# Two local attentions in one hand-ordered kernel: free tiles in place of a ring, first blocks in halves, new tables

## The chip, the core and the metric

One core of a Trainium2 chip runs the whole kernel. The metric is the device time of one execution in microseconds, as the median of several runs. TensorE multiplies matrices into PSUM, VectorE (DVE) and ScalarE (ACT) do elementwise work, GpSimd (POOL) masks and issues loads, SyncE (SP) issues DMAs.

## The reference

Two independent attention layers over 2048 positions and 1024 features, 32 heads of 32, whose outputs stand side by side. Layer A is dilated (8 keys, every second position), layer B a sliding window of 256 keys.

```python
def _A_ref(x, wqkv, wo):
    H = 32; W, dil = 8, 2
    q, k, v = heads(x @ wqkv)
    idx = pos[:, None] - (arange(W) * dil)[None, :]
    logits = einsum("bhsd,bhswd->bhsw", q, k[idx]) * Dh ** -0.5   # idx < 0 masked
    o = einsum("bhsw,bhswd->bhsd", softmax(logits), v[idx])
    return o.reshape(B, S, D) @ wo

def _B_ref(x, wqkv, wo):
    H = 32; W = 256
    q, k, v = heads(x @ wqkv)
    scores = einsum("bhqd,bhkd->bhqk", q, k) * Dh ** -0.5
    mask = (idx[:, None] - idx[None, :] >= 0) & (idx[:, None] - idx[None, :] < W)
    o = einsum("bhqk,bhkd->bhqd", softmax(where(mask, scores, -1e9)), v)
    return o.reshape(B, S, D) @ wo

return concatenate([a, b], axis=-1)
```

## The kernel before, in words

The work is cut into eight units of 512 positions: units 0 to 3 are layer B ("dense"), units 4 to 7 layer A ("window"), its even positions and its odd ones each in a row, so that the dilation is gone. A unit has eight head groups s of four heads. For each unit the kernel computes q and k of the eight groups (`qk_items`, L583), V in three parts (`v_items`, L648: one "wide" part of four groups and two parts of two), the attention of each group, and the output projection (`o_items`, L711), which runs during the next unit.

Everything is float32 through TensorE's rounded form: each operand is split into a high part and the low rest, and each product is three matmuls (`TERMS`). The split is made on the chip: `parts` casts the raw block to its high part on ScalarE (L208) or VectorE (L211), whichever the program expects to be done first, and subtracts for the low part on VectorE (L214).

**Blocks.** `Stream` holds a list of items, 512 KB each, in the order in which they are needed: x in four blocks of two tiles a unit, and the weights. The first six (`SIDE`) are loaded through SyncE, whole, and split in halves in an order written into `split_first`; the rest are loaded through GpSimd (L149) when one of three raw buffers falls free. Weights are split into a pool of three buffers, one or two blocks ahead of their use (`ahead`). In the wide part of V, four weight blocks are used one after the other for two column blocks b = 0 and 1; in dense units b = 1 runs two steps behind (`SKEW`). The split of the next block is begun with the first step of b = 1.

**Tiles.** x and the attention outputs `ot` share one pool of 19 tiles (`NX`) as a ring: each new tile takes the place of the one given out 19 tiles before (`Stream.tile`). Attention's values (`values_ready`, L835 and L1118) are not placed while that old tile is an output whose last projection hasn't run (`next_holds`).

**Attention of a dense group.** q and k leave PSUM as high and low parts (L520, L524) and six DMAs on SyncE scatter them into stacks of 96 rows, `qst` and `kst` (L544); k's last 256 positions go to HBM for the next unit (L534) and are read back there (L473). A first pass computes scores (L983), their maxima (L988) and sums (L993). Their logarithms go into rows 96 to 127 of the q stack (L1022, L1028), against ones in the same rows of the k stack, which `marks` writes once (L395). A second pass (L1067) gives probabilities by an exponential (L1074) and masks (L1052, L1055), and L1132 multiplies by V. Window groups have 64 small scores matmuls (L779), a softmax on VectorE and ScalarE (L787 to L830) and L851 for the values.

**The order of the work.** TensorE's order is written when the program is built. `Clock` models engines, queues and DMAs with fixed durations; the main loop at the end takes, at TensorE's modelled time, the first ready item of four lists: projections (`gemm`, with x's blocks as items of no cost), second passes, first passes and small ones. Tables steer it, one entry a unit. `V_AT` and `O_AT` say before which head group's q and k the parts of V and the projections of the unit before stand; `EDGES_V` says after how many steps at the end of a unit the next unit's blocks are split. `PACE` holds margins: for a dense unit the first number favours GpSimd for masks, the second is added to the modelled landing of k before scores may be placed, the third and fourth delay the second pass and the reuse of score banks, the fifth is added to the modelled cost of the values, the last says at which step of q and k the next weight is split:

```python
done["stack"][u, s] = max(e2, h2["hi"]) + PACE[u][1]
```

Constants are built at fixed modelled times: `turns` at 17, `keeps` at 23, `marks` (eight activations, four to each of the two k stacks) at 24, `nears` at 60. Ten warm-up matmuls (L1215) run before the first blocks land.

## Time and profile before

| | |
|---|---|
| median of 3 runs (lowest, highest) | 1802.55 us (1800.61, 1803.97) |
| the profiled execution | 1804.45 us |
| its span, first to last instruction | 1802.7 us |
| mean granted TensorE clock | 0.997 |
| GpSimd busy | 352.8 us (20%) |
| DMA, mean over the span | 143 GB/s, 257.52 MB |
| median from issue to landing, `raw` loads of wqk by GpSimd | 4.1 us |
| the same, k's scatter (`kst<-nat`) | 5.5 us |
| the same, the three whole x blocks on SyncE into `raw` | 7.5 us |

A row of the timeline gives start, duration, engine, line, operation, the tiles it writes and reads, shapes and count; in brackets stand the engine's idle time before it and what ended that. A row of waits gives who waited for whom, the total, the count and the longest. PE is TensorE, PEld its weight loads, which run beside it; SPq is SyncE's queue. Matmuls are pipelined and their ends modelled, so starts say more than durations.

### The profile page before, as it was taken

The page shows a single profiled execution, that of the slowest core. Times are in us where ns is not written, and L with a number is a line of the kernel's source. Part 1 is how long each engine was busy: PE and PEld are TensorE (multiplying, and loading weights), DVE is VectorE, ACT ScalarE, POOL GpSimd, SP SyncE. Part 2 cuts the span into 40 slices and gives each one's busy share as a digit, 9 for nine tenths or more (in the row PEclk, how much of TensorE's full clock was granted, in tenths as well). Part 3 has the DMA queues.
Part 4 walks back from the last instruction along what each step waited for, and adds up shares of the span by engine and source line. Part 5 has one row for each costly group of instructions (what it writes and reads, how often), then busy time and mean ns, then how long its engine had stood idle before and what let it go on. Part 6 is the DMA issues. An engine that isn't in the chain of part 4 may idle for free.

```text
span 1802.7 us, 39540 instructions
## 1 busy us (share of the span) xinstructions
PE 1778.2 (99%) x15210; PEld 1476.7 (82%) x15210; DVE 1270.3 (70%) x2757; ACT 1052.5 (58%) x2632; POOL 352.8 (20%) x759
## 2 busy tenths in 40 slices
PE   8999999999999999999999999999999999999999
PEld 6887888888788888888888888878888788888887
DVE  5778866649667678766667587787649576867783
ACT  5577676666666665757677455464525454644442
POOL 2111113232331212222242500110101000110000
PEclk9999999999999999999999999999999999999999
DMA  6555654546655556464545344444434443534432
GB/s 198 159 142 151 186 150 147 162 122 167 167 138 156 158 147 182 127 164 135 159 134 166 114 127 129 137 124 135 144 115 144 139 133 119 169 119 128 140 100 82
DMA packets 108860, 257.52 MB, mean 143 GB/s; under 512 B 14464, under 2 KB 29824, under 8 KB 108672
## 3 DMA queue, kind: packets, MB, share of 16 engines
q0 software_dynamic: 41760, 152.06, 28.3%
q1 hardware_dynamic: 57696, 86.15, 17.9%
q10 hardware_dynamic: 9216, 16.78, 2.5%
q8 instruction: 120, 1.97, 0.5%
q14 instruction: 68, 0.56, 0.1%
HBM read 164.63 MB, written 23.07 MB: 104 GB/s over the span
## 4 chain that ended last, share of the span: by engine, by line
PE 84%; DVE 6%; DMA 4%; ACT 3%; issue 2%; POOL 0%; SPq 0%; ACTq 0%; DVEq 0%; POOLq 0%
PE g L583 30%; PE g L711 14%; PE g L648 13%; PE s L1067 5%; PE x L583 5%; PE s L983 5%; PE x L711 4%; PE o L1132 3%; PE x L648 2%; DVE w L214 1%; PE s L779 1%; DMA halo<-nat 1%; ACT wide L827 1%; DMA kst<-nat 1%; DMA raw<-wqk 1%
## 5 line engine op out<-in xcount | busy, mean ns | idle before, releaser
L583 PE MATMUL g<-x,w 128*128 128x512 f32 x2640 | 659.7, 394 | 2.0 <-ACT w L208 1.6
L583 PEld LDWEIGHTS g<-x,w 128*128 128x128 f32 x2640 | 488.9, 189 | 96.5 <-ACT w L208 2.0
L988 DVE CUSTOM_DVE_ANT_0 s<-s,mask_d 128x384 f32<-128x384 f32 (+2 forms) x512 | 262.5, 555 | 133.0 <-PE s L983 132.3
L214 DVE TENSOR_TENSOR w<-raw,w 128x512 fp32r<-128x512 f32 x514 | 335.0, 694 | 25.3 <-ACT w L208 18.7
L648 PE MATMUL g<-w,x 128*128 128x256 f32 (+1 forms) x1920 | 347.6, 324 | 4.9 <-DVE w L214 3.1
L993 ACT ACTIVATE s<-s,nm 128x384 f32<-128x384 f32 (+2 forms) x512 | 273.7, 535 | 74.1 <-DVE nm L988 72.6
L648 PEld LDWEIGHTS g<-w,x 128*128 128x128 f32 x1920 | 286.9, 192 | 31.4 <-DVE w L214 5.4
L711 PE MATMUL g<-ot,w 128*128 128x512 f32 x1128 | 278.8, 392 | 0.0
L711 PEld LDWEIGHTS g<-ot,w 128*128 128x128 f32 x1128 | 208.8, 188 | 39.6 <-DVE ot L919 0.2
L1074 ACT ACTIVATE pbuf<-s 128x512 f32<-128x512 f32 (+1 forms) x368 | 189.3, 601 | 53.9 <-PE s L1067 46.3
L1052 POOL TENSOR_SCALAR_AFFINE_SELECT pbuf<-pbuf 128x256 f32<-128x256 f32 (+1 forms) x428 | 170.5, 425 | 212.3 <-ACT pbuf L1074 200.3
L211 DVE CAST w<-raw 128x1024 fp32r<-128x1024 f32 x191 | 136.9, 717 | 88.5 <-PE g L583 29.5
L149 POOL DMA_DIRECT2D raw<-wqk x126 | 69.1, 549 | 572.1 <-DVE w L214 341.3
L983 PE MATMUL s<-kst,qst 96*128 96x384 f32 (+2 forms) x512 | 144.2, 341 | 10.5 <-DMA halo<-nat 4.0
L1067 PE MATMUL s<-qst,kst 128*128 128x128 f32 (+2 forms) x704 | 128.5, 307 | 0.1
L827 ACT COPY wide<-wide 32x256 f32<-32x256 f32 x256 | 103.4, 404 | 34.1 <-DVE wide L818 30.4
L1067 PEld LDWEIGHTS s<-qst,kst 128*128 128x128 f32 x704 | 109.5, 189 | 16.8 <-ACT s L993 2.3
L983 PEld LDWEIGHTS s<-kst,qst 96*128 96x128 f32 x512 | 92.8, 190 | 33.9 <-ACT s L993 8.2
L993 ACT ACTIVATION_READ_ACCUMULATOR s<-s,nm 128x1 f32 x512 | 105.1, 205 | 0.1
L583 PE MATMUL x<-x,w 128*128 128x512 f32 x432 | 104.6, 394 | 0.0
L149 POOL DMA_DIRECT2D raw<-wv x72 | 46.7, 649 | 255.6 <-DVE w L214 131.3
L583 PEld LDWEIGHTS x<-x,w 128*128 128x128 f32 x432 | 80.0, 188 | 17.6 <-DVE w L214 0.4
(107 smaller groups left out, 1931.1 us busy)
## 6 DMA issues: line engine op xcount, KB each, us to landing
raw<-wqk POOLq DMA_DIRECT2D x126, 512.0 KB, 4.1
raw<-wv POOLq DMA_DIRECT2D x72, 512.0 KB, 4.3
raw<-wo POOLq DMA_DIRECT2D x64, 512.0 KB, 3.9
qst<-nat SPq DMA_DIRECT2D x96, 256.0 KB, 4.8
kst<-nat SPq DMA_DIRECT2D x96, 256.0 KB, 5.5
raw<-xs POOLq DMA_DIRECT2D x28, 512.0 KB, 4.9
outs<-ost ACTq DMA_DIRECT2D x56, 256.0 KB, 2.4
kst<-halo SPq DMA_DIRECT2D x72, 128.0 KB, 2.6
```

Source lines behind the costliest of these rows:

```text
L211: nc.vector.tensor_copy(t[:, 0, :], raw)
L214: nc.vector.tensor_tensor(t[:, 1, c:c + 512], raw[:, c:c + 512], t[:, 0, c:c + 512].bitcast(F32), op=ALU.subtract)
L583: nc.tensor.matmul(h["ps"], h["w"][:, a, k * P:(k + 1) * P], xt[u][k][:, b, :], start=(k == 0 and i == 0), stop=(k == NK - 1 and i == 2))
L648: nc.tensor.matmul(ps, xt[u][kw * g + k][:, a, p0:p0 + P], h["w"][g][:, c, k], start=(first and t == 0 and half == 0), stop=(last and t == 2),
L711: nc.tensor.matmul(h["ps"], w[:, a, c:c + P], ot[u, k][:, b, :], start=(k == 0 and i == 0), stop=(k == NK - 1 and i == 2))
L827: nc.scalar.copy(diag[r:r + 32, :, :, c:c + 32], pieces[r:r + 32, :, :, 1 + i % 2, :])
L983: nc.tensor.matmul(ps[:, :n], q[0:96, j, b * P:(b + 1) * P], kk[0:96, j, c0:c1], start=True, stop=True)
L988: nc.vector.tensor_tensor_reduce(ps[:, :n], ps[:, :n], mask[:, cut:full], scale=-1.0, scalar=BIG, op0=ALU.add, op1=ALU.min, accum_out=nm)
L993: nc.scalar.activation(ps[:, :n], ps[:, :n], AF.Exp, bias=nm, scale=-1.0, accum_out=sm)
L1052: nc.gpsimd.affine_select(w, w, pattern=[[0, m], [step, n]], compare_op=ALU.is_ge, fill=0.0, base=base, channel_multiplier=chan)
L1067: nc.tensor.matmul(ps[:, x:x + w], kk[:, j, 256 + kb * P:256 + (kb + 1) * P], q[:, j, q0:q0 + w], start=True, stop=True)
L1074: nc.scalar.activation(w, ps[:, :m * n].rearrange("p (j n) -> p j n", j=m), AF.Exp)
```

## The change

- `Tiles` replaces the ring: a list of free tiles. A tile of x is given back when its last matmul has been placed (`used` counts the steps that read it, 16 of q and k and 8 of V: `most`), a tile of `ot` with the last projection that reads it. `values_ready` asks for any free tile; an x item of units 1 to 7 for two.
- The twelve halves of the first six blocks are loaded one by one on SyncE, in the order `FIRST`, and `split_first` splits them in that order.
- `X_AT` lets the first blocks of the next unit's x stand ahead of a head group's q and k: in unit 0 block 0 before s = 6. (Unit 7 has an entry, but no next unit.)
- In the wide part of V, the split of the next weight begins with the first step of b = 0.
- The ones are written per k stack, at 5 and at 34 of the modelled time.
- `PACE`, `V_AT`, `O_AT` and `EDGES_V` get new entries.

```diff
...
+FIRST = ((0, 0), (1, 0), (0, 1), (2, 0), (3, 0), (3, 1), (4, 0), (1, 1), (4, 1), (2, 1), (5, 0), (5, 1))
+X_AT = ((6,), (), (), (), (), (), (), (6, 7))
...
-PACE = ((-0.2, 2.4, 0.1, 0.1, 0.0, -99, 4), (0.2, 1.2, 0.3, 0.1, 0.4, -99, 0), (0.1, 2.4, 0.3, 0.1, 0.0, -99, 0), (0.2, 1.2, 0.5, 0.4, 0.0, -99, 2), (6.0, 6.0, -0.5, 0.5, 1, 1), (4.0, 7.0, 1.5, 0.2, 1, 2), (4.0, 7.0, 0.5, 0.2, 1, 3), (4.0, 7.0, 0.5, 0.0, 1, 1))
-V_AT = ({0: 0, 4: 1, 7: 2}, {0: 0, 4: 1, 7: 2}, {0: 0, 5: 1, 7: 2}, {0: 0, 5: 1, 7: 2}, {1: 0, 5: 1, 7: 2}, {0: 0, 6: 1, 7: 2}, {0: 0, 5: 1, 7: 2}, {0: 0, 6: 1, 7: 2})
-O_AT = ({2: (0, 1), 3: (2, 3), 4: (4, 5), 5: (6, 7)}, {2: (0, 1), 3: (2, 3), 4: (4, 5), 5: (6, 7)}, {2: (0, 1), 3: (2, 3), 4: (4, 5), 5: (6, 7)}, {2: (0, 1), 3: (2, 3), 5: (4, 5), 6: (6, 7)}, {2: (0, 1), 3: (2, 3), 4: (4, 5), 6: (6, 7)}, {4: (0, 1), 5: (2, 3), 6: (4, 5), 7: (6, 7)}, {1: (0, 1), 2: (2, 3), 5: (4, 5), 6: (6, 7)}, {1: (0, 1), 2: (2, 3), 4: (4, 5), 5: (6, 7)})
+PACE = ((0.4, 2.4, 0.1, 0.1, 0.4, -99, 4), (0.1, 1.8, 0.3, 0.1, 0.4, -99, 2), (0.1, 0.6, 0.3, 0.1, 0.0, -99, 0), (0.2, 2.4, 0.3, 0.1, 0.0, -99, 0), (6.0, 8.0, 0.2, 0.5, 1, 1), (2.0, 6.0, 1.5, 0.2, 1, 2), (4.0, 7.0, 0.5, 0.2, 1, 3), (4.0, 7.0, -0.5, 0.0, 1, 1))
+V_AT = ({0: 0, 4: 1, 7: 2}, {0: 0, 3: 1, 7: 2}, {0: 0, 5: 1, 7: 2}, {0: 0, 5: 1, 7: 2}, {0: 0, 4: 1, 7: 2}, {0: 0, 6: 1, 7: 2}, {0: 0, 6: 1, 7: 2}, {0: 0, 6: 1, 7: 2})
+O_AT = ({2: (0, 1), 3: (2, 3), 4: (4, 5), 5: (6, 7)}, {3: (0, 1), 4: (2, 3), 5: (4, 5), 7: (6, 7)}, {2: (0, 1), 3: (2, 3), 4: (4, 5), 5: (6, 7)}, {2: (0, 1), 3: (2, 3), 4: (4, 5), 6: (6, 7)}, {3: (0, 1), 4: (2, 3), 5: (4, 5), 6: (6, 7)}, {2: (0, 1), 3: (2, 3), 4: (4, 5), 5: (6, 7)}, {1: (0,), 2: (1,), 3: (2, 3), 4: (4,), 5: (5,), 6: (6, 7)}, {1: (0,), 2: (1, 2), 3: (3, 4), 5: (5, 6), 6: (7,)})
...
-EDGES_V = (((2, 'k7'), (7, 'v0'), (14, 'x0'), (17, 'v1'), (17, 'q0'), (24, 'x1'), (28, 'x2'), (31, 'x3')), ((1, 'k7'), (4, 'x0'), (10, 'v0'), (11, 'v1'), (21, 'x1'), (23, 'x2'), (26, 'q0'), (31, 'x3')), ((2, 'k7'), (10, 'v0'), (14, 'v1'), (16, 'x0'), (22, 'x1'), (26, 'x2'), (26, 'q0'), (31, 'x3')), ((5, 'k7'), (7, 'v0'), (12, 'x0'), (17, 'v1'), (17, 'q0'), (18, 'x1'), (22, 'x2'), (26, 'x3')), ((2, 'k7'), (8, 'x0'), (10, 'v0'), (18, 'v1'), (20, 'x1'), (25, 'x2'), (26, 'q0'), (31, 'x3')), ((2, 'k7'), (7, 'v0'), (11, 'x0'), (14, 'v1'), (17, 'q0'), (18, 'x1'), (22, 'x2'), (26, 'x3')), ((0, 'k7'), (10, 'v0'), (11, 'x0'), (14, 'x1'), (15, 'v1'), (24, 'x2'), (29, 'q0'), (31, 'x3')), ((2, 'k7'), (7, 'v0'), (14, 'x0'), (17, 'v1'), (17, 'q0'), (21, 'x1'), (25, 'x2'), (29, 'x3')))
+EDGES_V = (((2, 'k7'), (5, 'v0'), (14, 'q0'), (17, 'x0'), (18, 'v1'), (27, 'x1'), (29, 'x2'), (33, 'x3')), ((1, 'k7'), (1, 'x0'), (10, 'v0'), (11, 'v1'), (20, 'x1'), (23, 'x2'), (32, 'q0'), (33, 'x3')), ((3, 'k7'), (10, 'v0'), (14, 'v1'), (15, 'x0'), (22, 'x1'), (26, 'x2'), (27, 'q0'), (31, 'x3')), ((5, 'k7'), (6, 'v0'), (12, 'x0'), (14, 'q0'), (17, 'v1'), (18, 'x1'), (24, 'x2'), (32, 'x3')), ((2, 'k7'), (5, 'x0'), (10, 'v0'), (16, 'v1'), (17, 'x1'), (22, 'x2'), (26, 'q0'), (28, 'x3')), ((0, 'k7'), (7, 'v0'), (13, 'x0'), (14, 'v1'), (17, 'q0'), (20, 'x1'), (26, 'x2'), (31, 'x3')), ((2, 'k7'), (10, 'x0'), (10, 'v0'), (15, 'v1'), (16, 'x1'), (26, 'x2'), (29, 'q0'), (33, 'x3')), ((2, 'k7'), (7, 'v0'), (14, 'x0'), (17, 'v1'), (17, 'q0'), (21, 'x1'), (25, 'x2'), (29, 'x3')))
...
+ONES_AT = 5.0, 34.0
...
+class Tiles:
+    def __init__(self, pool, ck):
+        self.pool, self.ck, self.free = pool, ck, list(range(NX))
+        self.seat, self.uses = {}, {}
+    def take(self, key, name="x"):
+        i = self.free.pop(0)
+        self.seat[key] = i
+        return self.pool.tile([P, 2, S], F32R, tag=f"x{i}", name=name)
+    def used(self, key, most):
+        n = self.uses[key] = self.uses.get(key, 0) + 1
+        if n == most:
+            self.ck.defer(self.ck.now + 0.2, lambda: self.free.append(self.seat[key]))
 class Stream:
...
-        self.ring = []
-        self.load_to(NRAW + len(more))
+        for i in range(SIDE):
+            self.raw[i] = (more[i] if i < len(more) else self.raws.tile([P, 1024], F32, tag="raw", name="raw")), [None, None]
+        for i, h in FIRST:
+            raw, ts = self.raw[i]
+            nc.sync.dma_start(raw[:, h * S:h * S + S], items[i][1][:, h, :] if items[i][0] == "x" else items[i][1][:, h * S:h * S + S])
+            ts[h] = ck.copy("half", ck.now)
+        self.loaded = SIDE
...
     def load_to(self, n):
...
-            early = self.loaded < SIDE
-            raw = self.more[self.loaded] if self.loaded < len(self.more) else self.raws.tile([P, 1024], F32, tag="raw", name="raw")
+            raw = self.raws.tile([P, 1024], F32, tag="raw", name="raw")
...
-            (self.nc.sync if early else self.nc.gpsimd).dma_start(raw if len(ap.shape) == 2 else raw.rearrange("p (a b) -> p a b", a=2), ap)
-            self.raw[self.loaded] = raw, (self.ck.copy if early else self.ck.fetch)("load", self.ck.now)
+            self.nc.gpsimd.dma_start(raw if len(ap.shape) == 2 else raw.rearrange("p (a b) -> p a b", a=2), ap)
+            self.raw[self.loaded] = raw, self.ck.fetch("load", self.ck.now)
...
-                    t = self.tile(None)
-                    self.ready[i].append(self.parts(t, raw[:, h * S:(h + 1) * S], t0, i < SIDE))
+                    t = self.seats.take(self.items[i][3] + (h,))
+                    self.ready[i].append(self.parts(t, raw[:, h * S:(h + 1) * S], t0, False))
...
-                self.ready[i] = self.parts(t, raw, t0, i < SIDE)
+                self.ready[i] = self.parts(t, raw, t0, False)
...
     def split_first(self):
...
-        for i, (kind, _, _) in enumerate(self.items[:SIDE]):
-            self.tiles[i] = [] if kind == "x" else self.wpool.tile([P, 2, 1024], F32R, tag="w", name="w")
+        for i in range(SIDE):
+            self.tiles[i] = [] if self.items[i][0] == "x" else self.wpool.tile([P, 2, 1024], F32R, tag="w", name="w")
...
-        for i, h in ((0, 0), (0, 1), (1, 0), (2, 0), (3, 0), (3, 1), (1, 1), (2, 1), (4, 0), (4, 1), (5, 0), (5, 1)):
+        for i, h in FIRST:
...
-                self.tiles[i].append(self.tile(None))
+                self.tiles[i].append(self.seats.take(self.items[i][3] + (h,)))
...
-            self.ready[i].append(self.parts(dst, raw[:, c], t, True))
+            self.ready[i].append(self.parts(dst, raw[:, c], t[h], True))
...
-    def tile(self, what):
-        self.ring.append(what)
-        return self.xpool.tile([P, 2, S], F32R, tag="x", name="x" if what is None else "ot")
-    def next_holds(self):
-        return self.ring[len(self.ring) - NX] if len(self.ring) >= NX else None
...
     def parts(self, t, raw, t0, side):
...
         for s in range(NG):
             if u and s in O_AT[u]:
...
+            plan += [("xe", u + 1, g) for g, at in enumerate(X_AT[u]) if at == s and u + 1 < U]
...
-        return [(at, keys.get(name) or ("x", u + 1, int(name[1]))) for at, name in (EDGES_V if with_v else EDGES_K)[EDGE_AT[u]]]
+        return [(at, keys.get(name) or ("x", u + 1, int(name[1]))) for at, name in (EDGES_V if with_v else EDGES_K)[EDGE_AT[u]]
+                if name[0] != "x" or int(name[1]) >= len(X_AT[u])]
...
+        elif p[0] == "xe":
+            unit_x(p[1], p[2])
...
+    most = [2 * NG + sum(n for _, n in parts_of(u)) for u in range(U)]
+    seats_x = Tiles(xpool, ck)
...
-    def marks():
+    def marks(t):
...
-        for t in kst:
-            for j in range(4):
-                nc.scalar.activation(t[96:P, j, :].rearrange("p (a s) -> p a s", s=P), zero, AF.Identity,
-                                     bias=heads[96:P, j:j + 1], scale=1.0)
-                ck.use("act", 0.73, ck.now)
+        for j in range(4):
+            nc.scalar.activation(t[96:P, j, :].rearrange("p (a s) -> p a s", s=P), zero, AF.Identity,
+                                 bias=heads[96:P, j:j + 1], scale=1.0)
+            ck.use("act", 0.73, ck.now)
...
+                seats_x.used(("x", u, k // 2, k % 2), most[u])
...
+            seats_x.used(("x", u, (kw * g + k) // 2, k % 2), most[u])
...
             if wide and r == 0:
-                if k == 0 and b == 1 and n < 3:
+                if k == 0 and b == 0 and n < 3:
...
+            if n == NG - 1:
+                seats_x.used(("ot", u, k), 1)
...
-        return [[(lambda: 0.0, lambda g=g: run(g), 0.0, lambda: None)] for g in range(4)]
+        def ready():
+            return 0.0 if not u or len(seats_x.free) > 1 else None
+        return [[(ready, lambda g=g: run(g), 0.0, lambda: None)] for g in range(4)]
...
         def values_ready():
-            if st.next_holds() is not None and (st.next_holds(), NG - 1) not in done["out"]:
+            if not seats_x.free:
...
-        o = st.tile(u)
+        o = seats_x.take(("ot", u, s), "ot")
...
-        o = st.tile(u)
+        o = seats_x.take(("ot", u, s), "ot")
...
         def values_ready(li):
-            if li and st.next_holds() is not None and (st.next_holds(), NG - 1) not in done["out"]:
+            if li and not seats_x.free:
...
     def insert(new, u):
-        xs_ = x_items(u + 1)
+        xs_ = xs_of[u + 1]
...
+    xs_of = [x_items(u) for u in range(U)]
...
-        if p[0] == "qk":
+        if p[0] == "xe":
+            gemm += xs_of[p[1]][p[2]]
+        elif p[0] == "qk":
...
-                q, k, x = new[:NK], new[NK:], x_items(0)
+                q, k, x = new[:NK], new[NK:], xs_of[0]
...
     causal()
-    for at, f in ((17.0, turns), (23.0, keeps), (24.0, marks), (60.0, nears)):
+    for at, f in ((ONES_AT[0], lambda: marks(kst[0])), (17.0, turns), (23.0, keeps), (ONES_AT[1], lambda: marks(kst[1])), (60.0, nears)):
...
```

10 lines of the change are left out of this document (5 added, 5 removed).

## The prediction

> **What bounds the kernel now.** I read the page first, then TensorE's own waits, then the timeline of each place that those waits point to. The page's engine rows and its chain:
>
> ```profile
> PE 1778.2 (99%) x15210; PEld 1476.7 (82%) x15210; DVE 1270.3 (70%) x2757; ACT 1052.5 (58%) x2632; POOL 352.8 (20%) x759
> ```
>
> ```profile
> PE 84%; DVE 6%; DMA 4%; ACT 3%; issue 2%; POOL 0%; SPq 0%; ACTq 0%; DVEq 0%; POOLq 0%
> ```
>
> TensorE is busy in 1778.2 of 1802.7 us, and the chain of work that ended last is TensorE for 84%. The change leaves its instructions what they are (no matmul is added or removed in the diff), so the most that it can win is TensorE's idle time, 24.5 us, and the time in which its clock was lower. The profiled execution took 1804.45 us, 1.75 us of it outside the span; the median of the three runs shown is 1802.55, 1.9 us less, and I carry every difference over to that median. Measured times of one kernel here lie within about 0.2% (3.6 us), and a smaller difference can't be told from none.
>
> TensorE's waits by what ended them (total, count, longest):
>
> ```profile
> PE s L983 <- DMA halo<-nat: 4.0, 3, 2.1
> PE s L983 <- DMA kst<-nat: 3.9, 3, 2.3
> PE g L648 <- DVE w L214: 3.1, 4, 1.3
> ```
>
> Three kinds matter: the first scores of a head group wait for q and k to land from their scatter DMAs (7.9 us; I read the first two rows as one kind, since the code issues the halo's store right behind the k scatter); V's matmuls wait for a split weight; the first matmul waits for the first blocks, as the timeline of the start shows, with a row of the last projections for comparison:
>
> ```profile
> 0.81 0.40 SPq L149 DMA_DIRECT2D pbuf<-xs  x1
> 5.24 1.14 ACT L208 CAST x<-pbuf 128x512 fp32r<-128x512 f32 x2 [3.15 <-DMA pbuf<-xs]
> 7.13 7.17 PE L583 MATMUL g<-x,w 128*128 128x512 f32 x22 [1.62 <-ACT w L208]
> 7.77 0.62 ACT L208 CAST w<-pbuf 128x512 fp32r<-128x512 f32 x1 [0.69 <-DMA pbuf<-wqk]
> ```
>
> ```profile
> 1782.57 11.04 PE L711 MATMUL g<-ot,x 128*128 128x512 f32 x48
> ```
>
> The view of windows gives, after each stretch and its length, the busy time of TensorE, its weight loads, VectorE, ScalarE and GpSimd, then the granted clock, the share of the DMA engines and GB/s:
>
> ```profile
> 4.64:8.05 3.41, 1.79 (x7) 0.86 (x6) 1.92 (x3) 2.03 (x4) 0.00 (x0) 1.00 1.03 411
> 8.05:11.46 3.41, 3.41 (x9) 2.63 (x9) 2.44 (x4) 2.74 (x6) 0.14 (x1) 0.50 0.76 311
> ```
>
> The reader sees 22 matmuls take 7.17 us where steady ones take 0.23 each: from 8.05 to 11.46 the clock was 0.50. In the window of 3.41 us ahead of it TensorE was idle for 3.41-1.79 = 1.62 us. The same happens twice more:
>
> ```profile
> 178.72:182.13 3.41, 0.87 (x6) 0.77 (x7) 3.38 (x6) 0.81 (x4) 1.06 (x2) 1.00 1.06 332
> 182.13:185.55 3.42, 3.42 (x18) 3.42 (x18) 1.75 (x12) 1.50 (x8) 0.00 (x0) 0.50 0.69 238
> 482.51:485.92 3.41, 1.53 (x7) 0.93 (x5) 1.89 (x7) 2.86 (x10) 0.00 (x0) 1.00 1.05 312
> 485.92:489.33 3.41, 3.18 (x8) 2.73 (x9) 1.25 (x4) 0.00 (x0) 0.00 (x0) 0.50 0.12 49
> 1185.10:1188.50 3.40, 2.13 (x10) 1.44 (x8) 3.40 (x7) 2.58 (x8) 0.00 (x0) 1.00 0.56 166
> 1188.50:1191.90 3.40, 3.36 (x63) 2.58 (x70) 1.89 (x3) 2.59 (x9) 1.12 (x2) 1.00 0.47 124
> ```
>
> Idle time of 1.62, 1.88 and 2.54 us in a window is followed by half clock for one window, 1.27 us (at 1185) is not. So here a wait beyond some 1.3 to 1.6 us costs itself and half of 3.41, 1.7 us, behind it. The Trainium skill ("TensorE: Matmul & The Clock Gate", "What's actually happening") lowers the clock after at least one idle window of about 3.4 us. No wait here is that long: the trace goes against the rule, and by it removing these waits would bring 1.7 us less at each place.
>
> **The change part by part.** What follows the first blocks now:
>
> ```profile
> 18.87 0.60 ACT L520 ACTIVATE nat<-g 128x512 fp32r<-128x512 f32 x1 [5.54 <-PE g L583]
> 19.50 1.33 SPq L544 DMA_DIRECT2D qst<-nat  x2
> 20.86 6.70 ACT L395 ACTIVATE kst<-mask_d,heads 32x768 fp32r<-32x768 f32 x8
> 21.47 0.68 DVE L211 CAST w<-raw 128x1024 fp32r<-128x1024 f32 x1
> 22.19 1.29 DVE L214 TENSOR_TENSOR w<-raw,w 128x512 fp32r<-128x512 f32 x2
> 22.21 0.51 PE L648 MATMUL g<-w,x 128*128 128x512 f32 x1 [0.30 <-DVE w L211]
> 23.54 10.02 PE L648 MATMUL g<-w,x 128*128 128x512 f32 x41 [0.82 <-DVE w L214]
> 34.45 0.63 PE L983 MATMUL s<-kst,qst 96*128 96x128 f32 x4 [0.89 <-DMA kst<-nat]
> ```
>
> *First blocks in halves.* Six loads of 512 KB on SyncE become twelve of 256 KB, in the order in which they are split. The first block is issued at 0.81 and split from 5.24; the third (k's weights, split at 7.77 right after its landing) has come 2.53 us later, so a block takes 1.27 us of transfer and a half 0.63. The first half of x then lands at about 4.6 and the first half of q's weights with the 512 KB that used to be x, at 5.2. Its cast takes 0.62, and the first matmul starts at 5.9 in place of 7.13: 1.25 us. Bounds: smaller blocks may move more slowly, down to nothing gained; at best the idle 1.62 us, since the warm-up matmuls fill the time before. SyncE issues six more times at 0.40 us; its next work is at 19.50, so that is covered. The Trainium skill ("DMA: Bandwidth & Descriptors", "Measured (HBM→SBUF, 128 partitions, SWDGE, issued from GpSimd)") speaks against halves: 1 MB transfers reach 78% of the peak, 64 KB 32%. By the trace the loads of one queue overlap (411 GB/s in the window from 4.64), so I keep the gain; no run here shows a half.
>
> The idle time in the window falls to 0.4 us, below 1.27, so the half clock goes too: 1.7 us. Against it: the splits behind. The low parts are one per half on VectorE, of the width of V's at 22.19, 1.29 for two, so twelve take 7.7 us and end by about 13.5, ahead of TensorE, which needs 48 x 0.23 = 11.0 us from 5.9 on. I allow 0.5 us of small waits. By 20.25, where V begins now, 1.25+1.7-0.5 = 2.45 us are won.
>
> *The first V part and the ones in k's pad rows.* V's second weight is cast at 21.47, behind the low parts of q and k, since its split is begun with the part's fourth step of three matmuls. Now it is begun with the first, 9 x 0.23 = 2.1 us sooner, and ScalarE is free of the eight activations of 20.86 (0.84 us each): four move into its hole of 5.54 us before 18.87, where they take 3.35, four to about 34 on the program's own clock. I drop both waits, 1.1 us. Bound on the other side: four activations in the first softmax, 3.35 us, if V's remaining matmuls did not cover them (about half of the part's 96 are left at 34.45, by the counts of the rows); I take 0. The wait of 0.89 for the k scatter stays: everything behind moves forward together. At the first scores the sum is 2.45+1.1 = 3.5 us, bounds 1 and 5.
>
> *V's split sooner elsewhere.* Three more waits of this kind, with VectorE's work ahead of one:
>
> ```profile
> 480.78 1.42 PE L648 MATMUL g<-w,x 128*128 128x512 f32 x5 [0.27 <-DVE w L214]
> 1184.82 1.84 DVE L818 STREAM_TRANSPOSE wide<-band 128x768 f32<-128x768 f32 x2
> 1187.22 1.27 DVE L214 TENSOR_TENSOR w<-raw,w 128x512 fp32r<-128x512 f32 x2
> 1188.54 0.74 PE L648 MATMUL g<-w,x 128*128 128x512 f32 x2 [1.31 <-DVE w L214]
> 1381.97 1.20 PE L648 MATMUL g<-w,x 128*128 128x512 f32 x4 [0.67 <-DVE w L214]
> ```
>
> In the window units the two column blocks aren't skewed, and sooner means one step, 0.7 us. That removes 0.27, 0.67, and 0.7 of 1.31: 1.6 us in all. Bounds: 2.25, and 0 if the low part stands in VectorE's queue behind the same softmax work (here behind two transposes, 1.84 us). The weight buffer is no new wait: the fourth weight overwrites the first, whose last reader stands ahead in TensorE's order.
>
> *Free tiles in place of the ring, and x's first block of unit 1 before step 6.* The same tiles hold the same data; there is no instruction more. What a free list changes is when x's splits and attention's values may be placed: `values_ready` waits for any free tile, x's item for two; while that item waits, the program places no matmul of the projections behind it, which shows as another order and not as a wait of an engine. Only unit 0 takes a block of x ahead (its load, two casts and two subtractions on ScalarE and VectorE); in unit 7 there is no next unit. It takes GpSimd's issue and the transfer out of the crowd at the end of unit 0, where the longest wait is:
>
> ```profile
> 180.71 0.63 PE L983 MATMUL s<-kst,qst 96*128 96x128 f32 x4 [2.32 <-DMA kst<-nat]
> 466.37 0.94 PE L983 MATMUL s<-kst,qst 96*128 96x384 f32 x4 [1.09 <-DMA halo<-nat]
> 486.15 0.66 PE L983 MATMUL s<-kst,qst 96*128 96x384 f32 x1 [2.12 <-DMA halo<-nat]
> 561.71 0.77 PE L983 MATMUL s<-kst,qst 96*128 96x384 f32 x3 [0.71 <-DMA kst<-nat]
> ```
>
> Which unit a place belongs to, by the count of L983's matmuls up to it (16 to each of a unit's eight head groups, 128 to a unit):
>
> ```profile
> 0.00:180.00 180.00, 23.57 (x96) 16.92 (x96) 0.99 0.58 162
> 0.00:466.00 466.00, 63.79 (x240) 42.92 (x240) 0.99 0.58 161
> 0.00:486.00 486.00, 68.75 (x256) 45.72 (x256) 0.99 0.58 162
> ```
>
> *Tables anew.* PACE's second number is the margin that the program leaves between its planned landing of k and the scores. It stays 2.4 in unit 0 (180.71), goes from 1.2 to 1.8 in unit 1 (466.37), from 2.4 to 0.6 in unit 2 (486.15, its first head group, and 561.71), and from 1.2 to 2.4 in unit 3. By that alone: 0.6 us won in unit 1, up to 1.8 lost at two places in unit 2. At 180.71 fewer transfers compete: 0 to 2.32 us won, and 1.7 of clock. O_AT, V_AT and EDGES move whole rows of matmuls: nothing by themselves, as TensorE has as many either way, and another set of waits, which I can only bound by the idle time now there beside the waits quoted here (24.5-12.1 = 12.4 us, the ends of the span among it): some 3 us either way. I take 1 us won for this group, between 8.4 won (0.6, and both large waits with their half clocks) and 8 lost (3.6, one more half clock, and those 3), because more of its margins grow than shrink and the largest wait is the one relieved.
>
> The sum: 3.5+1.6+1.0 = 6.1 us; 1804.45 becomes 1798.3, and the median 1796.5.
>
> **The rivals.**
>
> *The edges are cured.* The waits at 180.71 and 486.15 go (2.32+2.12) with both half clocks (3.4) and the rest as forecast but for its 1.0: 3.5+1.6+7.8 = 12.9 us, 1789.6. For it: in both windows the DMA share is over 1.0 (1.06 and 1.05), so transfers set those waits, and moving loads can cure them. Against: unit 2's margin was cut.
>
> *Won at the start, given back in the middle.* The two places in unit 2 wait 1.8 longer each, V's sooner splits hide nothing: 3.5-3.6 = 0, with a window of clock saved or not, 1801 to 1803; I put it at 1801.5. This takes in that the free list does nothing, which its use in one unit alone speaks for.
>
> *Slower: the margin of unit 2.* With 0.6 us left the scores of its eight head groups are placed before k has landed; TensorE runs its queue in order, so V's and the projections' matmuls behind the scores wait too. Each such place costs 1.8, and where that takes a window over 1.3 to 1.6 us of idle time, 1.7 of clock: 3.5. It decides from two places (7.0 against 5.1 won elsewhere); three give 5.4 us slower, 1808.0. For it: two places of unit 2 waited even with 2.4. Against: six such waits in the 32 groups of all four units.
>
> **How the numbers follow.** Forecast 0.45, its own range 1792 to 1800; edges cured 0.17; given back 0.24; slower 0.14. Faster by over 0.2% is below 1798.9: nine tenths of the forecast (0.41), all of the second case and a little of the third, 0.60; within it 0.27; slower 0.13. The range reaches from 1787.5, a little under the cured case, to 1805, over all of the third.
>
> **What would show it.** First real matmul near 5.9 us; no window of clock 0.50 in the first 20 us; V's second weight cast before the first part needs it, with no wait of L648's line on VectorE before 35 us; the first scores near 31 us; fewer than 0.5 us of such waits in units 5 and 6. For the middle, the granted clock at the end of unit 0 and at the start of unit 2 tells the cases apart. A first matmul after 6.6 us, or the half clock still behind it, would make the start wrong; more than three waits of the scores for k in unit 2 would make the slower case right.

## The result, and the profile after

The changed kernel takes 1791.58 us (median of 6 runs, 1790.76 to 1796.87) where the kernel before takes 1802.74 in the runs beside it: a ratio of 0.9945, with a 95% interval of 0.9929 to 0.9961. That is 11.2 us less, and 4.9 us below the forecast median. The profiled execution took 1790.78 us, its span 1789.1 us, 13.6 us less than the span before.

The engine rows and the chain of the page after:

```profile
PE 1770.9 (99%) x15210; PEld 1471.6 (82%) x15210; DVE 1274.8 (71%) x2751; ACT 1051.0 (59%) x2625; POOL 361.5 (20%) x772
```

```profile
PE 88%; DVE 4%; ACT 3%; DMA 3%; issue 1%; POOL 0%; SPq 0%; DVEq 0%; POOLq 0%; ACTq 0%
```

TensorE runs the same 15,210 matmuls and is idle for 1789.1 - 1770.9 = 18.2 us where it was 24.5. Its busy time fell by 7.3 us, most of it by the clock. Before, three windows of 3.41 us ran at 0.50, together 10.2 us that did the work of 5.1; after, no such window lies among TensorE's matmuls. So 6.3 us of the 13.6 are idle time and 5.1 are clock; the 2.2 us left are busy time at full clock, whose cause stays open. The two profiled executions lie 2.5 us further apart than the medians.

TensorE's waits after, first rows:

```profile
PE s L1014 <- DMA kst<-nat: 3.9, 2, 2.3
PE g L673 <- DVE w L233: 3.5, 4, 1.0
PE s L1014 <- ACT s L1024: 1.6, 4, 0.6
...
PE x L673 <- DVE w L233: 0.9, 1, 0.9
```

L1014 is the scores' line (L983 before), L673 V's (L648), L233 the low part's (L214). The scores' six waits for q and k, 7.9 us, have become two of 3.9 in all. V's waits for its split weights have not fallen: they were 3.1 us for low parts and 0.3 for a cast, and are now 3.5 and 0.9 (the first and the last row). Where the idle time went is read from the view of windows (the length, then TensorE's busy time; the difference is idle). Before:

```profile
0.00:40.00 40.00, 34.67 (x135) 26.46 (x136) 20.61 (x45) 21.09 (x43) 12.09 (x38) 0.96 0.70 217
40.00:150.00 110.00, 108.76 (x777) 89.08 (x776) 86.14 (x263) 74.09 (x212) 16.74 (x36) 1.00 0.54 144
150.00:200.00 50.00, 47.04 (x343) 39.91 (x343) 43.65 (x134) 35.12 (x103) 8.71 (x17) 0.97 0.52 148
400.00:520.00 120.00, 115.82 (x871) 95.40 (x870) 87.12 (x222) 79.32 (x209) 36.34 (x82) 0.99 0.56 156
1000.00:1600.00 600.00, 596.99 (x5957) 494.32 (x5957) 433.28 (x659) 300.97 (x693) 75.67 (x135) 1.00 0.43 133
```

After:

```profile
0.00:40.00 40.00, 35.86 (x143) 27.44 (x144) 23.25 (x48) 21.42 (x42) 13.16 (x38) 1.00 0.69 217
40.00:150.00 110.00, 107.43 (x737) 87.53 (x735) 72.08 (x212) 71.75 (x206) 32.27 (x87) 1.00 0.54 145
150.00:200.00 50.00, 50.00 (x397) 42.75 (x396) 41.50 (x121) 38.66 (x112) 14.97 (x35) 1.00 0.61 161
400.00:520.00 120.00, 116.67 (x982) 97.18 (x981) 90.89 (x235) 82.44 (x208) 32.81 (x65) 1.00 0.61 169
1000.00:1600.00 600.00, 597.44 (x6025) 494.65 (x6024) 430.30 (x662) 299.79 (x691) 69.81 (x122) 1.00 0.44 135
```

Idle at the start, 0 to 40: 5.33 became 4.14. From 40 to 150: 1.24 became 2.57, so the start's idle gain is given back there. At the end of unit 0, 150 to 200: 2.96 became nothing, and the clock goes from 0.97 to 1.00. At the start of unit 2, 400 to 520: 4.18 became 3.33, with the clock from 0.99 to 1.00. In the window units, 1000 to 1600: 3.01 became 2.56. The stretches left out (200 to 400, 520 to 1000, 1600 to 1780) go from 1.53, 2.14 and 0.49 to 1.09, 0.64 and 0.

The timeline of the start after, the rows of ScalarE, VectorE and TensorE that answer to those of the forecast:

```profile
3.72 0.62 ACT L227 CAST x<-pbuf 128x512 fp32r<-128x512 f32 x1 [1.63 <-DMA pbuf<-xs]
4.33 0.62 ACT L227 CAST w<-pbuf 128x512 fp32r<-128x512 f32 x1
7.24 0.62 ACT L227 CAST w<-pbuf 128x512 fp32r<-128x512 f32 x1 [1.43 <-DMA pbuf<-wqk]
...
30.16 0.59 ACT L626 COPY vbuf<-g 128x512 f32<-128x512 f32 x1 [11.51 <-PE g L673]
...
31.96 3.40 ACT L419 ACTIVATE kst<-mask_d,heads 32x768 fp32r<-32x768 f32 x4
```

```profile
18.68 0.69 DVE L548 SCALAR_TENSOR_TENSOR nat<-g,nat 128x512 fp32r<-128x512 f32 x1 [0.33 <-ACT nat L544]
19.29 0.68 DVE L230 CAST w<-raw 128x1024 fp32r<-128x1024 f32 x1
...
25.92 0.69 DVE L230 CAST w<-raw 128x1024 fp32r<-128x1024 f32 x1 [2.69 <-DMA raw<-wv]
```

```profile
1.52 4.64 PE L1249 MATMUL s<-qst 128*128 128x512 f32 x10 [1.52 <-DVE qst L1246]
5.95 1.68 PE L607 MATMUL g<-x,w 128*128 128x512 f32 x6
7.91 10.11 PE L607 MATMUL g<-x,w 128*128 128x512 f32 x42 [0.28 <-ACT w L227]
18.41 2.12 PE L673 MATMUL g<-w,x 128*128 128x512 f32 x7 [0.39 <-DVE nat L548]
21.36 5.81 PE L673 MATMUL g<-w,x 128*128 128x512 f32 x24 [0.83 <-DVE w L233]
28.00 2.13 PE L673 MATMUL g<-w,x 128*128 128x512 f32 x8 [0.83 <-DVE w L233]
29.96 0.56 PE L1014 MATMUL s<-kst,qst 96*128 96x128 f32 x4
```

The first half of x is split at 3.72 (the whole block at 5.24), the first matmul starts at 5.95 and 48 of them take 12.1 us without a slow window. L1249 are the ten warm-up matmuls. V begins at 18.41 (20.25 before) but still waits twice for low parts of its weights.

### The profile page after: what moved, and what is told of

Same layout as the page of the kernel before. It is cut to its first block, busy times and chain, and to the rows that moved or that the text cites. A ratio compares the mean times of both kernels' runs of the same rounds, so it can differ in the third digit from the quotient of the medians.

```text
span 1789.1 us, 39515 instructions
## 1 busy us (share of the span) xinstructions
PE 1770.9 (99%) x15210; PEld 1471.6 (82%) x15210; DVE 1274.8 (71%) x2751; ACT 1051.0 (59%) x2625; POOL 361.5 (20%) x772
## 4 chain that ended last, share of the span: by engine, by line
PE 88%; DVE 4%; ACT 3%; DMA 3%; issue 1%; POOL 0%; SPq 0%; DVEq 0%; POOLq 0%; ACTq 0%
PE g L607 31%; PE g L737 14%; PE g L673 14%; PE s L1098 6%; PE x L737 5%; PE x L607 5%; PE s L1014 5%; PE o L1163 3%; PE x L673 2%; PE s L810 1%; DVE w L233 1%; PE x L1163 1%; DMA kst<-nat 1%; DMA raw<-wv 1%; PE s L882 1%
## 5 line engine op out<-in xcount | busy, mean ns | idle before, releaser
L233 DVE TENSOR_TENSOR w<-raw,w 128x512 fp32r<-128x512 f32 x514 | 336.4, 696 | 38.9 <-ACT w L227 32.4
L673 PE MATMUL g<-w,x 128*128 128x256 f32 (+1 forms) x2016 | 353.6, 320 | 4.8 <-DVE w L233 3.5
L673 PEld LDWEIGHTS g<-w,x 128*128 128x128 f32 x2016 | 296.2, 190 | 32.7 <-DVE w L233 5.6
L737 PE MATMUL g<-ot,w 128*128 128x512 f32 x1080 | 265.5, 392 | 0.0
L737 PEld LDWEIGHTS g<-ot,w 128*128 128x128 f32 x1080 | 200.1, 188 | 39.3
L1083 POOL TENSOR_SCALAR_AFFINE_SELECT pbuf<-pbuf 128x256 f32<-128x256 f32 (+1 forms) x441 | 181.7, 437 | 216.8 <-ACT pbuf L1105 207.2
L230 DVE CAST w<-raw 128x1024 fp32r<-128x1024 f32 x188 | 130.9, 696 | 67.9 <-PE g L607 20.2
L1014 PE MATMUL s<-kst,qst 96*128 96x384 f32 (+2 forms) x512 | 145.3, 339 | 6.0 <-DMA kst<-nat 3.9
L1014 PEld LDWEIGHTS s<-kst,qst 96*128 96x128 f32 x512 | 92.4, 189 | 27.9 <-issue 6.4
L176 POOL DMA_DIRECT2D raw<-wo x64 | 34.7, 542 | 313.5 <-DVE w L233 149.3
```

Source lines behind the costliest of these rows:

```text
L176: self.nc.gpsimd.dma_start(raw if len(ap.shape) == 2 else raw.rearrange("p (a b) -> p a b", a=2), ap)
L230: nc.vector.tensor_copy(t[:, 0, :], raw)
L233: nc.vector.tensor_tensor(t[:, 1, c:c + 512], raw[:, c:c + 512], t[:, 0, c:c + 512].bitcast(F32), op=ALU.subtract)
L673: nc.tensor.matmul(ps, xt[u][kw * g + k][:, a, p0:p0 + P], h["w"][g][:, c, k], start=(first and t == 0 and half == 0), stop=(last and t == 2),
L737: nc.tensor.matmul(h["ps"], w[:, a, c:c + P], ot[u, k][:, b, :], start=(k == 0 and i == 0), stop=(k == NK - 1 and i == 2))
L1014: nc.tensor.matmul(ps[:, :n], q[0:96, j, b * P:(b + 1) * P], kk[0:96, j, c0:c1], start=True, stop=True)
```

## The experiments

Two explanations stood after the result. By the first, each edit carries its own share: the halves and the sooner split at the start, the tables at the edges of the units. By the rival, one of the two groups carries all of it. The third, that they are worth something only together, stands in part in the second run's expectation; it was taken up when the first two runs had failed both of the others.

**The parts without the tables.** The changed kernel with the four old tables and no x block ahead:

```diff
-PACE, V_AT, O_AT, EDGES_V = (new entries)
-X_AT = ((6,), (), (), (), (), (), (), (6, 7))
+PACE, V_AT, O_AT, EDGES_V = (entries of before)
+X_AT = ((),) * 8
```

> The changed kernel with the four tables of before and no block of x ahead: halves, V's split one step sooner, the ones in two lots and the free tiles alone. My theory is that the tables carry most of the gain and that the other parts keep little of what they win in the first 40 us: 1797 to 1803 us, against 1802.7 before and 1791.6 after. The rival, that these parts carry it and the tables only follow them: 1790 to 1795 us.

Measured: 1814.80 us against 1803.77, a ratio of 1.0059 (1.0046 to 1.0072).

**The tables without the parts.** The kernel before with the four new tables:

```diff
-PACE, V_AT, O_AT, EDGES_V = (entries of before)
+PACE, V_AT, O_AT, EDGES_V = (new entries)
```

> The kernel of before with the new PACE, V_AT, O_AT and EDGES_V alone: ring, whole first blocks, V's split late, the ones in one lot. If the tables carry most of the gain: 1792 to 1797 us. If the tables were fitted to the other parts and are worth nothing without them: 1800 to 1806 us.

Measured: 1814.95 us, 1.0057 (1.0045 to 1.0069). Both halves of the change are slower than before by some 11 us, and together they are faster by 11. No sum of separate shares gives that, and neither group carries the gain; both times lie outside every range that was expected. The idle time by stretch, at the end of this section, shows where each half loses.

**Whole first blocks, same order.** The changed kernel, its first six blocks loaded whole; the program goes on reckoning with halves, so TensorE's written order stays the same:

```diff
-            nc.sync.dma_start(raw[:, h * S:h * S + S], items[i][1][:, h, :] if ...)
+            if not h: nc.sync.dma_start(raw if items[i][0] == "w" else raw.rearrange("p (a b) -> p a b", a=2), items[i][1])
```

> The changed kernel with the first six blocks loaded whole, everything else issued in the same order on TensorE, VectorE, ScalarE and GpSimd. The first real matmul should go from 5.95 back to about 7.1 us and the half clock of 8 to 11.5 us should return, so that V begins some 2.3 us later. If the gain of the halves is given back by the waits behind it, the two traces meet again by 120 us and the time is 1791 to 1793 us. If it reaches the end: 1793.5 to 1796 us.

Measured: 1796.22 us, 0.9954 (0.9940 to 0.9967). Its timeline of TensorE:

```profile
7.18 13.03 PE L607 MATMUL g<-x,w 128*128 128x512 f32 x48 [1.75 <-ACT w L227]
34.76 0.71 PE L1014 MATMUL s<-kst,qst 96*128 96x128 f32 x4 [3.40 <-DMA kst<-nat]
```

The first matmul is back at 7.18, with the half clock behind it (7.87 to 11.28), and since the written order puts fewer of V's matmuls ahead of the first scores, these now wait 3.40 us for k. Up to 40 us TensorE is idle for 7.87 us where the halves leave 4.14. By the ratios to the kernel before, each beside its own run of it (0.9954 here, 0.9945 twice for the changed kernel), whole blocks cost 1.6 us, with intervals that overlap. So the halves are shown to win at the start; at the end they are worth a few us at most, and not the larger part of the gain: 8 us of it are there without them.

**More warm-up before.** The kernel before with 17 warm-up matmuls in place of ten, which takes its half clock at the start away and nothing else:

```diff
-        for i in range(WARM):
+        for i in range(WARM + 7):
```

> The kernel of before with 17 warm-up matmuls in place of 10, so that TensorE is busy until the first block is split, at about 7.1 us; nothing else is issued in another order. If idle time of 1.3 to 1.6 us in a window of 3.41 us lowers the clock, no 0.50 shows before 20 us and the time falls by 1.7 us, to 1801. If the half clock follows only from a whole idle window or belongs to the start, it stays and the time is 1802.7 or a little more.

Measured: 1803.88 us, 0.9998 (0.9987 to 1.0008). The timeline:

```profile
1.52 6.89 PE L1215 MATMUL s<-qst 128*128 128x512 f32 x17 [1.52 <-DVE qst L1212]
8.25 11.06 PE L583 MATMUL g<-x,w 128*128 128x512 f32 x48
```

The 48 matmuls take 11.06 instead of 13.06, so the clock was what made them slow. But the warm-up ends late, the first matmul starts 1.1 us later, and of 0.9 us won at V's beginning (19.37 against 20.25) nothing can be measured at the end: the expected 1801 us didn't come.

**The changed kernel again**, as a control:

> The changed kernel as it is, on one chip with the three that follow, so that they have something to be compared with: 1790 to 1797 us, with the single times spread by how many windows of half clock a run draws (1.7 us each and what they upset).

Measured: 1794.22 us (1789.56 to 1797.98), 0.9945 (0.9932 to 0.9959). The ratio repeats.

**The ring, all else as changed.** The tiles are given out as a ring again:

```diff
-        i = self.free.pop(0)
-        return self.pool.tile([P, 2, S], F32R, tag=f"x{i}", name=name)
+        self.ring.append(key[1] if name == "ot" else None)
+        return self.pool.tile([P, 2, S], F32R, tag="x", name=name)
...
-            if not seats_x.free:
+            if seats_x.full(done["out"]):
```

> The changed kernel with the ring put back in place of the free tiles; the block of x ahead, the halves, V's earlier split, the ones in two lots and the new tables stay. TensorE's order is the same up to the second unit and differs in patches from there. If the free tiles are a means of letting the tables place work and little else: 1791 to 1795 us. If they carry the gain of 11 us: 1799 us or more.

Measured: 1813.20 us, 1.0046 (1.0033 to 1.0058). Up to 400 us its idle time is that of the changed kernel to 0.5 us. From 400.5 us on TensorE's order parts from it. The first large wait, on TensorE, on ScalarE and in SyncE's queue:

```profile
434.44 1.65 PE L673 MATMUL g<-w,x 128*128 128x256 f32 x6 [4.49 <-DVE nat L548]
```

```profile
433.06 0.60 ACT L544 ACTIVATE nat<-g 128x512 fp32r<-128x512 f32 x1 [4.32 <-DMA qst<-nat]
```

```profile
423.62 1.89 SPq L568 DMA_DIRECT2D qst<-nat  x3
425.61 2.26 SPq L568 DMA_DIRECT2D kst<-nat  x3
```

V's matmuls need a bank that holds q or k; ScalarE, which empties it, waits for the buffer that an earlier scatter is still reading. In the changed kernel the scatters of this place stand some 8 us sooner in SyncE's queue:

```profile
415.37 1.88 SPq L568 DMA_DIRECT2D qst<-nat  x3
417.34 2.60 SPq L568 DMA_DIRECT2D kst<-nat  x3
```

The wait costs 4.49 us, and from 431.86 on the clock is halved for 6.83 us. Three more follow, ending at 962 (3.15 us), 1194 (2.04) and 1404 (3.27), the last with a half clock too. That a ring must have such waits is not shown, since the tables were not made for it.

**One table or part taken back at a time**, in the changed kernel: the old `PACE`; the old `EDGES_V`; the ones' second lot at 21 in place of 34; V's split as late as before; no block of x ahead in unit 0.

> The changed kernel with the PACE of before alone (margins 1.2, 2.4, 1.2 for units 1 to 3 in place of 1.8, 0.6, 2.4). If the tables are fitted as one set to one plan, a margin put back makes the other tables wrong from the first unit on: 1797 to 1806 us. If each table does its own work, PACE has a part of it: 1792 to 1796 us. My forecast's fear, that a margin of 0.6 in unit 2 costs waits, would show as a time below 1790.

> The changed kernel with the EDGES_V of before alone (at which step at a unit's end the next unit's blocks are split). If the set is fitted as one: 1797 to 1806 us, with the new waits at the ends of units. If each table does its own work: 1793 to 1797 us. If the edges do nothing: as the changed kernel.

```diff
-ONES_AT = 5.0, 34.0
+ONES_AT = 5.0, 21.0
```

> The changed kernel with the second lot of ones at 21 in place of 34 of the modelled time, in ScalarE's hole of 11.5 us ahead of 30.16 and out of the first softmax. By its own account 0.7 us of waits at 35.4 and 36.0 go: 1791 us. If any shift near the start makes the fitted set wrong: 1797 to 1806 us.

```diff
-                if k == 0 and b == 0 and n < 3:
+                if k == 0 and b == 1 and n < 3:
```

> The changed kernel with V's next weight split from the first step of the second column block, as before. By my forecast's term 1.6 us slower, 1793 to 1796 us, with waits of V's matmuls for a low part as in the profile before. If the set is fitted as one: 1797 to 1806 us.

```diff
-X_AT = ((6,), (), (), (), (), (), (), (6, 7))
+X_AT = ((),) * 8
```

> The changed kernel without the block of x ahead of unit 0's seventh head group: all four blocks of unit 1's x are split at the end of unit 0. If the block relieves the end of unit 0, the wait of 2.3 us for k that the profile before had near 180 us comes back, with a draw of half clock: 1794 to 1799 us. If it does nothing: as the changed kernel, 1791 to 1794 us.

**Larger margins at the two waits that are left.** The scores of unit 0's second group and of unit 1's seventh are placed 2.0 and 2.6 us later:

```diff
-                        done["stack"][u, s] = max(e2, h2["hi"]) + PACE[u][1]
+                        done["stack"][u, s] = max(e2, h2["hi"]) + PACE[u][1] + {(0, 1): 2.0, (1, 6): 2.6}.get((u, s), 0.0)
```

> The changed kernel with 2.0 us more margin for the scores of unit 0's second head group and 2.6 us more for unit 1's seventh, the two places that wait 1.8 and 2.3 us for k to land in the profile after; TensorE's order differs in patches only. If such a wait can be mended where it stands: 3 to 4 us faster than the changed kernel, 1787 to 1791 us, and no draw of half clock there. If other waits take their place: 1791 to 1797 us.

What these six measured, with the other runs. The stretches hold TensorE's idle us (length less busy time, by the view of windows), "half" is the time at half clock up to the last matmul. "Order" is taken from the traces: of the 15,210 matmuls in TensorE's sequence, how many are left over when as many as possible are matched, in order and by their line in the kernel, with those of the changed kernel. The medians come from different groups of runs and are compared by the ratios.

| kernel | median us | ratio to before (95%) | order | 0-40 | 40-150 | 150-200 | 200-400 | 400-520 | 520-1000 | 1000-1600 | half |
|---|---|---|---|---|---|---|---|---|---|---|---|
| before | 1802.74 | 1 | | 5.3 | 1.2 | 3.0 | 1.5 | 4.2 | 2.1 | 3.0 | 10.2 |
| changed | 1791.58 | 0.9945 (0.9929-0.9961) | 0 | 4.1 | 2.6 | 0 | 1.1 | 3.3 | 0.6 | 2.6 | 0 |
| changed, again | 1794.22 | 0.9945 (0.9932-0.9959) | 0 | 3.9 | 2.8 | 0 | 1.1 | 3.5 | 0.9 | 2.5 | 3.4 |
| two margins | 1792.52 | 0.9939 (0.9926-0.9951) | 150 | 5.9 | 1.8 | 0 | 1.1 | 0.9 | 0.2 | 3.1 | 6.8 |
| whole blocks | 1796.22 | 0.9954 (0.9940-0.9967) | 0 | 7.9 | 3.5 | 0 | 1.1 | 3.4 | 1.1 | 2.6 | 10.2 |
| no x ahead | 1794.61 | 0.9957 (0.9944-0.9971) | 422 | 4.2 | 2.4 | 1.1 | 3.1 | 1.0 | 0.8 | 2.8 | 0 |
| old PACE | 1804.32 | 1.0004 (0.9995-1.0013) | 1396 | 4.5 | 1.8 | 0.5 | 3.4 | 1.0 | 6.1 | 5.9 | 10.2 |
| ones at 21 | 1803.61 | 1.0004 (0.9995-1.0014) | 632 | 4.0 | 7.7 | 1.4 | 4.6 | 0.9 | 0.8 | 2.5 | 10.2 |
| old EDGES_V | 1806.60 | 1.0020 (1.0011-1.0029) | 879 | 4.7 | 3.1 | 0.2 | 3.0 | 2.1 | 3.0 | 6.0 | 10.2 |
| V's split late | 1807.95 | 1.0024 (1.0012-1.0037) | 988 | 4.6 | 3.1 | 0 | 2.8 | 3.5 | 3.4 | 6.9 | 10.2 |
| ring | 1813.20 | 1.0046 (1.0033-1.0058) | 779 | 3.7 | 3.0 | 0 | 1.1 | 6.3 | 4.8 | 7.3 | 10.2 |
| parts alone | 1814.80 | 1.0059 (1.0046-1.0072) | | 4.5 | 1.4 | 3.1 | 2.2 | 3.2 | 4.0 | 8.4 | 13.7 |
| tables alone | 1814.95 | 1.0057 (1.0045-1.0069) | | 5.8 | 1.6 | 0.8 | 2.8 | 5.5 | 3.1 | 7.8 | 20.5 |

The stretches are those of one profiled execution each, and such a one can lie some us from its median (ring 1807.83 us, whole blocks 1800.30).

Three things follow. First, five of the seven edits that let the program write another order lose the whole gain or more, whatever it was that was taken back. That is what "fitted as one" had expected; `EDGES_V` and V's split late lie 0.6 and 2.0 us above its range. Their losses lie far from the edit. With V's split late, TensorE's order is that of the changed kernel up to 208 us, and up to 200 us the run is idle for 0.9 us more (7.65 against 6.71); in the window units it is idle for 6.9 against 2.6 us. The ones are moved at 21 to 34 us and the idle time comes from 107 us on, first in the middle of unit 0:

```profile
112.72 0.98 PE L673 MATMUL g<-w,x 128*128 128x256 f32 x6 [3.38 <-DVE nat L548]
```

What is lost is idle time, at the edges of units and elsewhere, and the half clock that it draws (10.2 us in the profile of each of the five). So the tables fit the order that this very set gives, and not the edits one by one. That a plan made of fixed durations answers a small edit with a new order, and that such orders were tried until one with few waits was found, is how I explain it; no run shows how the tables were found. The edits that move few matmuls (150 and 422) keep the gain, those that move 632 and more lose it; among these the loss doesn't follow the number (1396 moved: 1804.3 us, 779: 1813.2). An edit of no meaning that moves as many was not run, so how much of a loss is the edit's own and how much that of any new order stays open.

Each group alone loses mostly in the window units too: the parts alone are idle there for 8.4 us and keep the wait at unit 0's end (3.1); the tables alone are idle there for 7.8, for 5.5 at the start of unit 2, and keep the old start (5.8).

Second, the edge of unit 0 (150 to 200) is cured by the tables: 3.0 before and 3.1 with the parts alone, 0.8 with the tables alone, at most 1.4 in every kernel that has most of them. Neither the block of x ahead nor one of `PACE` and `EDGES_V` is needed for it: without the block the expected wait of 2.3 us for k near 180 us doesn't come back.

Third, taking the two waits left away with larger margins gives nothing that can be measured at the end (0.9939 against 0.9945), though the trace gains. TensorE's waits in that run, and a row of its start:

```profile
PE g L673 <- DVE w L233: 4.0, 6, 1.0
PE g L673 <- DVE w L230: 1.7, 1, 1.7
PE s L1249 <- DVE qst L1246: 1.5, 1, 1.5
PE g L673 <- DVE nat L548: 1.5, 2, 1.1
```

```profile
29.14 0.49 PE L673 MATMUL g<-w,x 128*128 128x512 f32 x1 [1.75 <-DVE w L230]
```

No scores wait for `kst` any more (3.9 us less), and from 40 us on TensorE is idle for 7.1 us where the changed kernel is for 10.2. V's weights are waited for 2.2 us longer (5.7 in place of 3.5), 1.7 of it at 29 us, with a half clock behind it. But that place stands ahead of the edit: TensorE's order is the same up to 70.7 us. This execution had a weight block cast at 28.39, when it had landed, and the changed kernel's profile at 25.92, so the 1.7 us and the half clock are not the margins' work.

## Why the prediction was right

The median lies in the range, 4.9 us below the number and 0.4 below the forecast's own range; the rival in which the edges are cured, 1789.6, was nearer by its sum. By the sign that the forecast named, the granted clock at the end of unit 0 (0.97 to 1.00) and at the start of unit 2 (0.99 to 1.00), it was this rival, given 0.17, that came true in the middle. What bounds the kernel was read rightly: idle time of TensorE and the half clock behind it are 11.4 of the 13.6 us between the profiles. That the sum came near is in good part luck: two of its terms brought less than half of what was forecast, and the third, put at 1.0, stands for places that won 9.6.

- **The start.** First matmul at 5.95 (5.9 forecast), no half clock in the first 20 us: both as said, the first by luck. The blocks were there sooner (the cast of q's weights ends at 4.95), and the matmul stands behind the ten warm-up matmuls, which leave no idle time ahead of it. They took 4.64 us here and 3.99 in the profile before; with the old start and 4.63 (tables alone) TensorE was idle for 1.14 us and no half clock followed, so whether the old start draws the 1.7 us of clock is in part chance. The half of k's weights is split only at 7.24, so 0.28 us of wait follows, within the 0.5 allowed. V begins 1.84 us sooner, not 2.45.
- **V's waits in the first part** were dropped in the forecast, and that failed: the two of 0.30 and 0.82 became three, 0.39 for the low part of q or k (`nat`) and twice 0.83 for that of a weight. The weight's cast did move up, from 21.47 to 19.29, but it still stands behind q's and k's low parts (18.68) on VectorE, and ScalarE, free of the ones, is idle for the 11.51 us before 30.16: the split was not given to it. The last of the three is for a block that VectorE casts at 25.92, after 2.69 us of waiting for its load: there the split waits for the transfer, not for its place in the order.
- **First scores at 29.96**, 31 forecast, seems better than said. It isn't: 39 of V's matmuls stand ahead of them now and 48 did before, so 9 x 0.23 = 2.1 of the 4.5 us are order. The gain there is about 2.4 us, against 3.5 forecast.
- **The ones' second lot** was put at 0 with a bound of 3.35, and 0 holds: it runs at 31.96 to 35.36 on ScalarE, in the first softmax, and the scores' waits for ScalarE are 1.6 us in all.
- **What the start keeps.** The second group's scores now wait for k at 70.70, 1.61 us, and from 40 to 150 idle time grows from 1.24 to 2.57. The forecast named a giving back, for unit 2; it came in unit 0.
- **V sooner elsewhere, 1.6 us**: not won. The waits of 0.27, 1.31 and 0.67 (2.25 in all) gave way to others of the kind at 209 (0.83), 1370 (1.04) and 1564 (0.94), 2.81 in all, and the whole stretch 1000 to 1600 wins 0.45 us. "Fewer than 0.5 us of such waits" was wrong. The run with V's split late has the same 3.5 us of waits for low parts as the changed kernel, and 0.9 us more for casts; the sooner split takes away no more than that:

```profile
PE g L673 <- DVE w L233: 3.5, 4, 1.0
PE g L673 <- DVE w L230: 0.9, 3, 0.4
```

- **Tables, 1.0 us**: the term that failed in size. By the windows from 150 us on, without the window units, idle time fell by 2.96 at the end of unit 0, 0.85 from 400 to 520 and 2.4 in the rest; with two half clocks less, 3.4 us, these places won 9.6. The term's bound was 8.4. This counts by place: that the tables alone do it is refuted, since without the parts they are 11 us slower than before. The margin that was to cost up to 3.6 in unit 2 cost nothing: no scores of unit 2 wait for k, and the one new wait (2.33 at 430) is in unit 1, whose margin grew. The slower rival, which rested on that margin, fell with it.
- **Free tiles, nothing by themselves**: not settled as it was put. With everything else as changed, the ring is slower by 19 us, but the tables in it were not made for it; with the old tables free tiles are slower too. That free tiles gain by themselves was not shown, and neither was the opposite.
- **Where the gain lies.** 1.6 (start, less what is given back; 1.2 + 1.7 - 1.3) + 0.45 + 9.6 = 11.7 of the 13.6 us between the profiles; the 2.2 us of busy time at full clock, less 0.3 us at the ends of the span, are the rest.
- The forecast took the tables for entries that act one by one, each costed by its margin. The runs show a set: half of it is 11 us slower than before, the whole 11 us faster.

## What to carry to other kernels

Where the order of an engine is written by a program from modelled times, cost a change by the places it was fitted to (the waits at the edges and the clock behind them), and be ready for a single part of it, taken out or put in alone, to lose at places that it doesn't touch; five of seven did here. Measure such a change whole, and when one part is to be tried by itself, hold the written order fixed, as in the run with whole blocks. A gain at the start of a long kernel is to be followed up to a place well behind it before it is counted, and at equal work: an earlier first score can be fewer matmuls ahead of it.

## What the runs showed of the hardware

**The half clock follows idle time in a window of a grid, not the length of a wait.** The forecast had a wait beyond 1.3 to 1.6 us as what lowers the clock. The starts of the slow windows in one execution are whole multiples of 3.413 us apart (before: 8.05, 182.13, 485.92). In the profile after, counting back so from the one at 1788.01, behind the last matmul, the windows in which the two largest waits fall:

```profile
67.70:71.11 3.41, 1.79 (x11) 1.24 (x9) 0.72 (x2) 1.10 (x2) 0.00 (x0) 1.00 1.05 315
426.09:429.50 3.41, 1.85 (x14) 1.57 (x13) 1.71 (x4) 0.88 (x2) 0.39 (x1) 1.00 1.06 295
429.50:432.91 3.41, 2.64 (x56) 2.08 (x57) 1.14 (x4) 0.19 (x1) 0.00 (x0) 1.00 0.34 128
```

The same kernel's second profile, at the wait for k that is 1.61 us in the first and 1.86 here:

```profile
68.62:72.03 3.41, 1.55 (x9) 1.12 (x8) 0.86 (x7) 1.57 (x5) 0.00 (x0) 1.00 1.06 308
72.03:75.44 3.41, 3.41 (x11) 2.79 (x10) 2.60 (x10) 2.26 (x11) 0.00 (x0) 0.50 0.85 191
```

The wait of 2.33 us at 428 to 430 falls on a boundary, 1.56 us in one window and 0.77 in the next, and the clock stays at 1.00; at 2.32 us in one window (before, at 180) it had fallen. Idle 1.62 us at 67.70 does nothing, 1.62 at 4.64 before was followed by 0.50, 1.86 here too. Over the 14 profiles, with the grid laid out from the slow windows of each, every whole window at full clock with 1.85 us of idle time or more was followed by half clock, and none with less than 1.32. Between these both happen (1.32 in the parts alone, at 962, was followed; 1.79 with the old `PACE`, at 962, was not): the limit lies at about half a window, as well as modelled ends of matmuls allow. It doesn't tell how long the half clock lasts: with V's split late a second slow window follows one with 0.25 us of idle time. The grid's phase differs from run to run (a boundary at 71.11 in the first of these profiles, at 72.03 in the second), so one and the same wait can cost 1.7 us more in one execution than in another, as the wait for k near 70 us (1.61 and 1.86 us) did. From the limit of about 1.6 us in a window, waits of up to some 3.2 us can escape in this way; that length is an estimate. The Trainium skill ("TensorE: Matmul & The Clock Gate", "What's actually happening") has windows of this length that run freely, and the trace agrees (3.413 us); its condition of a whole idle window is more than these runs needed.

**Halves on one queue come sooner.** The first 256 KB are split from 3.72, the first 512 KB were from 5.24; over the profiles it is 3.72 to 4.80 in ten with halves and 5.24 to 5.37 in four with whole blocks. But the first half of k's weights, fourth in the queue now, is split at 7.24, and its whole block, third in the queue, was at 7.77: what is won is the first block, not the rate.
